# Four weight loads in place of nine, in a fused attention and feed-forward kernel

## The chip, the cores and the metric

The kernel runs on one core of a Trainium2 chip. The metric is the device time of one execution in microseconds (us), as the median of several runs. A core has TensorE (PE: matrix products), VectorE (DVE), ScalarE (ACT), GpSimd (POOL) and SyncE (SP), each with its own program in a fixed order, and 16 DMA engines that all of its queues share.

## The reference

All tensors are float32. There are 8 batches, 12 heads, 448 positions and 64 elements per head.

```python
def rmsnorm(x, g):
    return x / np.sqrt(np.mean(x * x, axis=-1, keepdims=True) + 1e-06) * g
q_n, k_n = rmsnorm(q, g_q), rmsnorm(k, g_k)
scores = np.matmul(q_n, k_n.transpose(0, 1, 3, 2)) / np.sqrt(64)
attn = exp(scores - max) / (sum of the row + 1e-9)
attn_out = np.matmul(attn, v)                                    # (8, 12, 448, 64)
x = attn_out.transpose(0, 2, 1, 3).reshape(3584, 768)
h = x @ w_in                                                     # w_in  (768, 2048)
g = h * np.clip(h + 3.0, 0.0, 6.0) / 6.0
out = g @ w_out                                                  # w_out (2048, 768)
```

## The kernel before

**Units of work.** Two heads make a pair; six pairs are a batch, 48 pairs in all, handled in order. Loads of q, k and v go by groups of two pairs (GP = 2): 384 KB for the first 384 positions of a tensor, in rows of 768 B, and smaller DMAs for the last 64 positions, in rows of 256 B. They land in rings of three groups (`kq_in`, `v_st`). After the first groups, SP issues all of them (L281 to L300), so that they share one hardware queue, which the profile calls q1.

**A pair's way through attention.** GpSimd squares q and k (L334; ScalarE does it for the first pairs), VectorE sums the squares (L337), ScalarE makes the reciprocal root for both pairs of a group (L345, L348), GpSimd normalizes into bf16 (`qk`, L353). The result is transposed: on TensorE for pairs 0 to 13 (L367, then copied by L385 and L303), by a DMA afterwards (L377). TensorE makes scores (L395, L402), ScalarE their exponentials (L408), TensorE the weighted sums of v (L429, L435), VectorE divides (L445, L446), and the result, transposed again, goes into `xT`.

**The feed-forward part.** For each batch, `h_item` makes 16 row blocks of h, transposed, with six products each (L479, 448 columns, over the six 128-row blocks of w_in). ScalarE (L485) and VectorE (L490) apply the gate and write `gT`. `y_item` makes output tiles: 16 products each over w_out's sixteen 128-row blocks (L498), 384 of the 768 columns at a time. One block of batch 0 (`h_early`) goes product by product as each pair's `xT` comes. The attention of the next batches and the feed-forward of the earlier ones are mixed on TensorE.

**What sets the order.** A planner (`Plan`) runs a small model of the engines while the kernel is built and puts every instruction into its engine's program. At run time each engine follows that order and waits where an operand is not there. The model books every DMA in one file, `pipe`: a DMA takes its size divided by RATE (270 bytes per ns) behind the one before it, and is taken to have landed LAND = 1700 ns later. `dma_transpose` books 1.4 times its size. An operation is placed when its operands are there by this model, by its key; feed-forward items fill TensorE by the shares in `share`.

**The weights.** They lie in HBM as float32 and are cast to bf16 by the DMA itself, issued by GpSimd (the software queue, q0). w_in comes by columns in five DMAs (256, 256, 512, 512 and 512 columns); w_out in four, each of eight 128-row blocks and one half of the columns. The lists say after which group's v load a DMA may be issued, and then columns or blocks:

```python
W_IN = ((2, 0, 256), (2, 256, 256), (2, 512, 512), (3, 1024, 512), (3, 1536, 512))
W_OUT = ((5, 0, 0, 8), (5, 0, 8, 8), (6, 1, 0, 8), (7, 1, 8, 8))
```

`h_item` waits for the w_in DMA that holds its 128 columns. `y_item` waits for the two DMAs of its half of w_out's columns, and for the first batch the output tiles stand in an order that uses the first half of the columns for two tiles before the second half.

Of the kernel before, what the change touches and what calls it, by code (L numbers as in the profile page):

```python
# [63 lines left out]
class Plan:  # L64
# [3 lines left out]

    HOP = 60
    PRICE, FAIR = {"POOL": 0.5, "ACT": 2.0, "DVE": 1.5}, 0  # L70
    ISSUE, LAND, RATE = {"SP": 600, "ACT": 600, "POOL": 900}, 1700, 270.0

    STEADY, SLACK, EARLY = 110e3, 500, 3000

# [6 lines left out]
    def add(self, key, ways, deps=(), lag=0, size=0, hold=False):  # L81
        op = Op(key, ways, deps, lag, size)
        op.left += hold
        self.todo += 1
        if op.left == 0:
            self.known.append(op)
        return op

    def dma(self, key, n, size, fn, deps=(), queue="SP", hold=False):

        op = self.add(key, [(queue, self.ISSUE[queue] * n, fn)], deps, self.LAND, size, hold)
        op.load = True
        return op

    def dma_transpose(self, key, size, fn, deps):
        return self.add(key, [("SP", 1270, fn)], deps, 2100, 1.4 * size)

    def item(self, lane, place, count, ns, fn, deps):

# [89 lines left out]
def kernel(  # L189
# [11 lines left out]
    nc = tc.nc  # L201

    B, H, S, D = q.shape
    DM, DFF = moe_w_in.shape
    P = 128
    NT = S // P
# [4 lines left out]
    NKT = DM // P  # L211
# [4 lines left out]
    GP = 2  # L216
    NV, NK, NX, NE, NQ = 4, 4, 3, 8, 3
    YC = 384
# [33 lines left out]
    w_out_sb = const.tile([P, NFT, DM], BF16, name="w_out_sb")  # L252
# [7 lines left out]
    plan = Plan(share=(2.0, 1.0, 0.65, 3.0, 0.45))  # L260
# [51 lines left out]
    def load_w_in(c, n):  # L312
        nc.gpsimd.dma_start(out=w_in_sb[:, :, c:c + n],
                            in_=moe_w_in[:, c:c + n].rearrange("(kt p) f -> p kt f", p=P))

    def load_w_out(half, f, n):
        cols = slice(half * YC, (half + 1) * YC)
        nc.gpsimd.dma_start(out=w_out_sb[:, f:f + n, cols],
                            in_=moe_w_out[f * P:(f + n) * P, cols].rearrange("(ft p) m -> p ft m", p=P))


    def which(part):
# [172 lines left out]
    def y_mm(b, t, c, n, f, m):  # L495

        c0 = (0 if b % 2 == 0 else S + REST) + t * P if t < NT else FULL
        nc.tensor.matmul(  # L498
            out=m[:, 0:n], lhsT=gT[:, f, c0:c0 + P], rhs=w_out_sb[:, f, c:c + n],
            start=(f == 0), stop=(f == NFT - 1),  # L500
        )

    def y_copy(eng, c, n, m, ys):
        copy(eng, out=y_r[ys][:, c:c + n], in_=m[:, 0:n])

    def y_store(b, t, ys, cols):
        y = y_r[ys][:, cols]
        if t < NT:
            rows = out[b * S:b * S + FULL, cols].rearrange("(p t) m -> p t m", t=NT)
            nc.sync.dma_start(out=rows[:, t, :], in_=y)  # L510
        else:
            nc.sync.dma_start(out=out[(b - 1) * S + FULL:b * S, cols], in_=y[0:REST])
            nc.sync.dma_start(out=out[b * S + FULL:(b + 1) * S, cols], in_=y[REST:P])
# [58 lines left out]
    h_ops, gates, y_ops, stores = {}, {}, {}, []  # L572

    def h_item(b, f):
        deps = [w_in_op(f)] + px[HP * b:HP * b + HP]

        deps += y_ops.get(b - 2, [])[-1:] + (y_rest.get(b - 1, []) if b % 2 == 0 else [])
        it = plan.item("h", b + f / NFT, NKT, 189, lambda kt, m: h_mm(b, f, kt, m), deps)
        h_ops.setdefault(b, []).append(it.ops[-1])
        n = len(gate_ops)  # L580
        t = t_r[n % len(t_r)]
        r = add((0, 0), [("ACT", 550, lambda: relu(it.bank[0], t))],
                [it.ops[-1]] + gate_ops[n - len(t_r):n - len(t_r) + 1] * (n >= len(t_r)))
        it.out = add((0, 0), [("DVE", 600, lambda: gate(b, f, it.bank[0], t))], [r])
        gates.setdefault(b, []).append(it.out)
        gate_ops.append(it.out)

    def h_early(f):

        m, t, mm = m_r[f], t_r[f], None  # L590
        for kt in range(NKT):
            mm = add((kt + 2, 2), [("PE", 189, lambda kt=kt: h_mm(0, f, kt, m))],
                     [px[kt], mm, w_in_op(f)], 165)
        h_ops.setdefault(0, []).append(mm)
        r = add((0, 0), [("ACT", 550, lambda: relu(m, t))], [mm])
        out = add((0, 0), [("DVE", 600, lambda: gate(0, f, m, t))], [r])
        gates.setdefault(0, []).append(out)
        gate_ops.append(out)
        plan.banks.append([m, out])

    def y_item(b, t, c, n, place, alone=False):

        part = c // YC
        deps = [*w_out_ops[part], *gates[b], *(gates[b - 1] if t == NT else [])]
        it = plan.item("y", place, NFT, 3 + n / 2.4, lambda f, m: y_mm(b, t, c, n, f, m), deps)
        y_ops.setdefault(b, []).append(it.ops[-1])
        if t == NT:
            y_rest.setdefault(b, []).append(it.ops[-1])
        if (b, t) not in y_rows:
            y_rows[b, t] = (len(y_rows), [])  # L610
        k, parts = y_rows[b, t]
        ys = k % len(y_r)
        it.out = add((0, 1), [("ACT", 160 + 0.83 * n, lambda: y_copy(A_, c, n, it.bank[0], ys)),
                              ("DVE", 160 + 1.04 * n, lambda: y_copy(V, c, n, it.bank[0], ys))],
                     [it.ops[-1]] + ([stores[k - len(y_r)]] if k >= len(y_r) else []))
        parts.append(it.out)
        if alone:
            plan.dma((-1, 0), 1, P * n * 4, lambda: y_store(b, t, ys, slice(c, c + n)), [it.out])
        elif len(parts) == DM // YC:
            stores.append(plan.dma((-1, 0), 1 if t < NT else 2, P * DM * 4,  # L620
                                   lambda: y_store(b, t, ys, slice(0, DM)), parts))

    def feed_forward(b):

        if b:
            ts = (NT, *range(NT)) if b % 2 == 0 else range(NT)
            ys = [(t, c) for t in ts for c in range(DM // YC)]
            if b == 1:
                ys = [(0, 0), (1, 0), (0, 1), (1, 1), (2, 0), (2, 1)]
            for i, (t, c) in enumerate(ys):  # L630
                last = b == B and t == NT - 1
                for j in range(2 if last and c else 1):
                    n = YC // 2 if last and c else YC
                    y_item(b - 1, t, c * YC + j * n, n, b + YLAG + (i + j / 2) / len(ys), last)
        if b < B:
            for f in range(NFT):
                h_early(f) if b == 0 and f < 1 else h_item(b, f)

    gate_ops, y_rows, y_rest = [], {}, {}
    QA, VL, WK = 1, 1.5, 0  # L640
    YLAG = 0.12


    W_IN = ((2, 0, 256), (2, 256, 256), (2, 512, 512), (3, 1024, 512), (3, 1536, 512))
    W_OUT = ((5, 0, 0, 8), (5, 0, 8, 8), (6, 1, 0, 8), (7, 1, 8, 8))
    w_loads, w_in_ops, w_out_ops = [], [], ([], [])
    for i, (after, *cols) in enumerate(W_IN):
        op = plan.dma((GP * after - WK, 3 + i), 1, NKT * P * cols[1] * 4, lambda cols=cols: load_w_in(*cols),
                      queue="POOL", hold=True)
        w_loads.append((after, op))  # L650
        w_in_ops.append((sum(cols), op))
    for i, (after, *rows) in enumerate(W_OUT):
        op = plan.dma((GP * after - WK, 8 + i), 1, rows[2] * P * YC * 4, lambda rows=rows: load_w_out(*rows),
                      queue="POOL", hold=True)
        w_loads.append((after, op))
        w_out_ops[rows[0]].append(op)

    def w_in_op(f):
        return next(op for end, op in w_in_ops if f * P < end)
# [16 lines left out]
    for p in range(NPAIR):  # L676
        g = p // GP
        if p % GP == 0:
# [6 lines left out]
            for p0, n in todo:  # L685
                lk.append(plan.dma((p0, 0), 3, n * kb, lambda p0=p0, n=n: load_k(nc.sync, p0, n), old))
                eng, queue = (nc.scalar, "ACT") if g < QA else (nc.sync, "SP")
                lq.append(plan.dma((p0, 1), 2, n * kb, lambda p0=p0, n=n, eng=eng: load_q(eng, p0, n), old,
                                   queue=queue))
# [10 lines left out]
            for i in range(GP):  # L700
                j, p0 = min(i, len(todo) - 1), p + i
                parts = []
                for part in ((0, 1) if p0 == 0 else (2,)):
                    m = len(squares)
                    n = 2 if part == 2 else 1
# [95 lines left out]
    x_stage(NPAIR - 1)  # L801
    plan.banks += [[x[:, 0], d_ops[i - 2]] for i, x in enumerate(sc_r)]
    feed_forward(B - 1)
    feed_forward(B)
    with tc.manual_schedule(engines=set(ENGINES.values())):
        plan.run()
# [31 lines left out]
```

## Time and profile before

| | |
|---|---|
| median of 3 runs | 439.57 us (438.73 to 439.68) |
| the profiled execution | 439.38 us, of which the span of the core 437.6 us |
| TensorE busy | 409.8 us (94% of the span) |
| ScalarE, VectorE, GpSimd busy | 254.3, 234.7, 195.2 us |
| DMA packets | 126506, 64.55 MB |
| software queue (q0, the weights) | 8144 packets, 6.29 MB, 9.2% of 16 engines' span |

The weight DMAs, as the trace has their issue (us from the span's start) and the time to landing:

| | issued at | us to landing |
|---|---|---|
| w_in columns 0 to 256, to 512, to 1024 | 28.7, 29.6, 30.4 | 8.3, 11.0, 15.8 |
| w_in columns to 1536, to 2048 | 35.5, 36.4 | 16.2, 21.6 |
| w_out, first half of the columns | 39.1, 40.0 | 25.0, 30.3 |
| w_out, second half of the columns | 63.6, 75.2 | 13.2, 10.7 |

In the slices of the page, 40 to the span, a digit is the busy share in tenths, 9 for 90% or more. A DMA's packets are told with the bytes that were written, so that a row of weights that is cast counts half of what is read. Times of packets of two queues on one engine can overlap: a share over 100% is possible. In a timeline row, "x2" means two instructions told together, with the time of both.

### The profile page before, as it was taken

How to read it: one execution, taken by the hardware profiler on the slowest of the kernel's cores; microseconds unless marked ns; L12 is line 12 of the kernel's file. 1: busy time of each engine (PE TensorE's matmuls, PEld its weight loads, DVE VectorE, ACT ScalarE, POOL GpSimd, SP SyncE). 2: the span in 40 equal slices, each digit the busy share in tenths (PEclk: the TensorE clock that was granted, in tenths of full speed). 3: DMA queues.
4: the chain of work that ended last, by engine and by line, in shares of the span. 5: the costliest groups of instructions: out<-in, count | busy, mean ns of one | idle time of the engine just before them, and what ended most of it. 6: DMA issues, size and time to landing. Idle time of an engine off the chain costs nothing.

```text
span 437.6 us, 8944 instructions
## 1 busy us (share of the span) xinstructions
PE 409.8 (94%) x3520; PEld 236.5 (54%) x3520; DVE 234.7 (54%) x492; ACT 254.3 (58%) x414; POOL 195.2 (45%) x146
## 2 busy tenths in 40 slices
PE   0677899999999998999999999999999999999997
PEld 0355565555566554555555555555565555555565
DVE  6486777766455557556466366344444253343322
ACT  3886887734877885968778587666643032132100
POOL 3697785596377776859676556311000000000000
PEclk9998999999999999999999999999999999999999
DMA  6999999995978898999999994333211201100022
GB/s 170 267 228 216 221 222 239 250 190 131 237 161 190 204 217 189 201 219 194 227 212 167 191 213 121 73 88 91 61 24 49 72 1 51 59 36 37 25 85 73
DMA packets 126506, 64.55 MB, mean 148 GB/s; under 512 B 77824, under 2 KB 123008, under 8 KB 126464
## 3 DMA queue, kind: packets, MB, share of 16 engines
q1 hardware_dynamic: 117488, 57.24, 57.5%
q0 software_dynamic: 8144, 6.29, 9.2%
q8 instruction: 27, 0.44, 0.4%
q10 hardware_dynamic: 832, 0.46, 0.4%
q14 instruction: 15, 0.12, 0.1%
HBM read 45.61 MB, written 11.01 MB: 129 GB/s over the span
## 4 chain that ended last, share of the span: by engine, by line
PE 82%; DMA 7%; ACT 3%; DVE 3%; SPq 2%; POOL 2%; issue 1%; ACTq 0%; POOLq 0%
PE m L479 18%; PE m L498 17%; PE t_ps L498 9%; PE t_ps L479 8%; PE av L435 7%; PE sc L395 6%; PE sc L498 6%; PE sc L479 4%; DMA kq_in<-in_k_dram 3%; DMA kq<-qk 3%; PE av L429 2%; DMA kq_in<-in_q_dram 2%; PE sc L402 2%; ACT eT L408 2%; DVE ssq L337 1%
## 5 line engine op out<-in xcount | busy, mean ns | idle before, releaser
L408 ACT ACTIVATE eT<-sc 128x896 bf16<-128x896 f32 x168 | 147.2, 915 | 42.2 <-PE sc L395 38.5
L498 PEld LDWEIGHTS <-gT 128*128 128x128 bf16 x912 | 85.5, 98 | 61.7 <-issue 8.9
L479 PE MATMUL m<-xT,w_in_sb 128*128 128x448 bf16 x486 | 109.9, 353 | 1.7 <-DVE xT L475 0.6
L479 PEld LDWEIGHTS <-w_in_sb 128*128 128x128 bf16 x768 | 70.7, 98 | 68.8 <-issue 12.0
L353 POOL TENSOR_TENSOR qk<-kq_in,rstd 128x1024 bf16<-128x1024 f32 x47 | 89.0, 1903 | 41.6 <-DMA kq<-qk 20.8
L498 PE MATMUL m<-w_out_sb,gT 128*128 128x384 bf16 (+1 forms) x480 | 87.3, 324 | 0.0
L334 POOL TENSOR_TENSOR sq<-kq_in 128x1024 f32<-128x1024 f32 x41 | 77.2, 1894 | 13.0 <-DMA kq_in<-in_q_dram 3.6
L490 DVE SCALAR_TENSOR_TENSOR gT<-t_sb,m 128x448 bf16<-128x448 f32 x81 | 49.9, 618 | 41.8 <-ACT t_sb L485 41.4
L485 ACT ACTIVATE t_sb<-m 128x448 f32<-128x448 f32 x81 | 44.1, 546 | 47.9 <-PE m L479 47.2
L337 DVE TENSOR_REDUCE ssq<-sq 128x16 f32<-128x1024 f32 (+1 forms) x49 | 58.1, 1190 | 9.5 <-POOL sq L334 7.5
L435 PE MATMUL av<-vaug,eT 128*128 128x65 bf16 x1152 | 59.6, 196 | 0.0
L435 PEld LDWEIGHTS <-eT 128*128 128x128 bf16 x1152 | 52.8, 100 | 7.2 <-issue 1.6
L498 PE MATMUL t_ps<-w_out_sb,gT 128*128 128x384 bf16 x256 | 46.9, 326 | 0.0
L395 PE MATMUL sc<-kq 64*128 64x448 bf16 x288 | 41.6, 363 | 4.0 <-ACT eT L408 2.5
L429 PE MATMUL av<-vaug,eT 128*128 128x130 bf16 x192 | 43.0, 224 | 2.4 <-ACT eT L408 1.2
L479 PE MATMUL t_ps<-xT,w_in_sb 128*128 128x448 bf16 x192 | 44.5, 352 | 0.7 <-DVE gT L490 0.7
L303 POOL CAST vaug<-v_st 128x512 bf16<-128x512 f32 x33 | 20.3, 620 | 55.0 <-PE av L435 46.6
L445 DVE RECIPROCAL rden<-av 128x4 f32<-128x4 f32 x96 | 17.3, 180 | 48.8 <-PE av L435 47.1
L446 DVE TENSOR_TENSOR xn<-av,rden 128x256 bf16<-128x256 f32 x96 | 40.7, 424 | 3.3
L374 ACT ACTIVATE kq<-kq,gprime 128x448 bf16<-128x448 bf16 x34 | 22.8, 670 | 14.2 <-DMA kq<-qk 14.2
L498 PE MATMUL sc<-w_out_sb,gT 128*128 128x384 bf16 (+1 forms) x176 | 29.1, 319 | 0.0
L485 ACT ACTIVATE t_sb<-t_ps 128x448 f32<-128x448 f32 x32 | 17.5, 547 | 19.7 <-PE t_ps L479 18.5
(50 smaller groups left out, 225.0 us busy)
## 6 DMA issues: line engine op xcount, KB each, us to landing
v_st<-in_v_dram SPq DMA_DIRECT2D x24, 384.0 KB, 4.7
kq_in<-in_k_dram SPq DMA_DIRECT2D x23, 384.0 KB, 4.5
kq_in<-in_q_dram SPq DMA_DIRECT2D x23, 384.0 KB, 4.8
out_dram<-y_sb SPq DMA_DIRECT2D x23, 384.0 KB, 2.6
w_out_sb<-in_moe_w_out_dram POOLq DMA_DIRECT2D x4, 768.0 KB, 19.1
w_in_sb<-in_moe_w_in_dram POOLq DMA_DIRECT2D x3, 768.0 KB, 16.2
out_dram<-y_sb SPq DMA_DIRECT2D x9, 192.0 KB, 2.7
v_st<-in_v_dram SPq DMA_DIRECT2D x48, 32.0 KB, 4.3
```

The source lines that it names most:

```text
L334: eng.tensor_tensor(out=sq, in0=x, in1=x, op=A_MULT)
L337: nc.vector.tensor_reduce(out=ssq_r[(p // GP) % 2][:, p % GP, :, which(part)].rearrange("p h a t -> p h (a t)"), in_=sq_r[m][:, :, which(p ...
L353: eng.tensor_tensor(out=qk_r[p % NQ][:].rearrange("p a t h d -> p h (a t) d"), in0=raw(p, 2), in1=rstd_r[(p // GP) % 2][:, p % GP].rearran ...
L395: nc.tensor.matmul(out=sc[:, h, 0:S], lhsT=kT_r[p % NK][rows, t * P:(t + 1) * P], rhs=qT_r[p % NK][rows], start=True, stop=True,)
L408: nc.scalar.activation(out=e2_r[d % NE][:, :, 0:S], in_=sc_r[i][:, :, 0:S], func=EXP, bias=0.0, scale=1.0,)
L429: nc.tensor.matmul(out=av, lhsT=rest[:, cols], rhs=va[:, 3].rearrange("p h d -> p (h d)"), start=True, stop=False, skip_group_check=True,)
L435: nc.tensor.matmul(out=av[:, h * W:(h + 1) * W], lhsT=e[t][h][:, cols], rhs=va[:, t, h], start=False, stop=(t == NT - 1 and h == 1), skip_ ...
L446: nc.vector.tensor_tensor(out=xn_r[p % NQ][:, t].rearrange("p n (h d) -> p n h d", h=2), in0=av4[:, :, :, 0:D], in1=rden.unsqueeze(3).to_b ...
L479: nc.tensor.matmul(out=m[:, 0:S], lhsT=w_in_sb[:, kt, f * P:(f + 1) * P], rhs=xT[:, kt, b % NX, x_slot(b)], start=(kt == 0), stop=(kt == N ...
L485: nc.scalar.activation(out=t[:], in_=m[:, 0:S], func=RELU, bias=0.5, scale=1.0 / 6.0,)
L490: nc.vector.scalar_tensor_tensor(out=gT[:, f, (b % 2) * S:(b % 2 + 1) * S], in0=t[:], scalar=1.0, in1=m[:, 0:S], op0=A_MIN, op1=A_MULT,)
L498: nc.tensor.matmul(out=m[:, 0:n], lhsT=gT[:, f, c0:c0 + P], rhs=w_out_sb[:, f, c:c + n], start=(f == 0), stop=(f == NFT - 1),)
```

## The change

Weights come in four DMAs: w_in in two halves of its columns (rows of 4096 B read, 2048 written), w_out in two halves of its row blocks with all columns (3072 B read, 1536 written). All of w_out may be issued after group 5. An output tile waits for both w_out DMAs, and the first batch's output tiles stand in the common order. The planner books 310 bytes per ns, 3000 ns more until a GpSimd DMA has landed, four fifths of the weights' size and 1.25 times that of a transpose.

```diff
-    ISSUE, LAND, RATE = {"SP": 600, "ACT": 600, "POOL": 900}, 1700, 270.0
+    ISSUE, LAND, RATE = {"SP": 600, "ACT": 600, "POOL": 900}, 1700, 310.0
+    SHARED = 3000
...
-        op = self.add(key, [(queue, self.ISSUE[queue] * n, fn)], deps, self.LAND, size, hold)
+        op = self.add(key, [(queue, self.ISSUE[queue] * n, fn)], deps, self.LAND + self.SHARED * (queue == "POOL"), size, hold)
...
-        return self.add(key, [("SP", 1270, fn)], deps, 2100, 1.4 * size)
+        return self.add(key, [("SP", 1270, fn)], deps, 2100, 1.25 * size)
...
-    def load_w_out(half, f, n):
-        cols = slice(half * YC, (half + 1) * YC)
-        nc.gpsimd.dma_start(out=w_out_sb[:, f:f + n, cols],
-                            in_=moe_w_out[f * P:(f + n) * P, cols].rearrange("(ft p) m -> p ft m", p=P))
+    def load_w_out(f, n):
+        nc.gpsimd.dma_start(out=w_out_sb[:, f:f + n, :],
+                            in_=moe_w_out[f * P:(f + n) * P, :].rearrange("(ft p) m -> p ft m", p=P))
...
-        part = c // YC
-        deps = [*w_out_ops[part], *gates[b], *(gates[b - 1] if t == NT else [])]
+        deps = [*w_out_ops, *gates[b], *(gates[b - 1] if t == NT else [])]
...
-            if b == 1:
-                ys = [(0, 0), (1, 0), (0, 1), (1, 1), (2, 0), (2, 1)]
...
-    W_IN = ((2, 0, 256), (2, 256, 256), (2, 512, 512), (3, 1024, 512), (3, 1536, 512))
-    W_OUT = ((5, 0, 0, 8), (5, 0, 8, 8), (6, 1, 0, 8), (7, 1, 8, 8))
-    w_loads, w_in_ops, w_out_ops = [], [], ([], [])
+    W_IN = ((2, 0, 1024), (3, 1024, 1024))
+    W_OUT = ((5, 0, 8), (5, 8, 8))
+    w_loads, w_in_ops, w_out_ops = [], [], []
...
-        op = plan.dma((GP * after - WK, 3 + i), 1, NKT * P * cols[1] * 4, lambda cols=cols: load_w_in(*cols),
+        op = plan.dma((GP * after - WK, 3 + i), 1, NKT * P * cols[1] * 4 * 4 // 5, lambda cols=cols: load_w_in(*cols),
...
-        op = plan.dma((GP * after - WK, 8 + i), 1, rows[2] * P * YC * 4, lambda rows=rows: load_w_out(*rows),
+        op = plan.dma((GP * after - WK, 8 + i), 1, rows[1] * P * DM * 4 * 4 // 5, lambda rows=rows: load_w_out(*rows),
...
-        w_out_ops[rows[0]].append(op)
+        w_out_ops.append(op)
```

## The prediction

> **What bounds the kernel now.** I read the page's engine totals first, then its slices, then the windows around the weight loads.
>
> ```profile
> PE 409.8 (94%) x3520; PEld 236.5 (54%) x3520; DVE 234.7 (54%) x492; ACT 254.3 (58%) x414; POOL 195.2 (45%) x146
> ```
>
> ```profile
> PE   0677899999999998999999999999999999999997
> ...
> DMA  6999999995978898999999994333211201100022
> ```
>
> TensorE is the bound: 409.8 of 437.6 us busy, 27.8 idle. The change leaves its work alone, so it can move the time only through that idle time. The DMA engines are full in the first 24 slices (to some 260 us). The weights travel between about 31 and 86 us, so I looked there, in windows of 10 us:
>
> ```profile
> core 0: us, PE busy (x) PEld busy (x) DVE busy (x) ACT busy (x) POOL busy (x), PEclk, DMA share, GB/s
> 30.00:40.00 10.00, 7.83 (x98) 5.27 (x96) 6.30 (x16) 6.35 (x12) 9.98 (x9) 0.83 1.17 203
> 40.00:50.00 10.00, 8.03 (x106) 5.16 (x105) 6.70 (x18) 8.22 (x13) 6.54 (x6) 1.00 1.19 224
> 50.00:60.00 10.00, 9.50 (x108) 5.67 (x107) 8.21 (x19) 8.18 (x14) 7.44 (x7) 1.00 1.21 221
> ```
>
> TensorE idles 2.17 + 1.97 + 0.50 = 4.6 us here, and is full afterwards, but for 2.9 us between 160 and 180 and 1.2 between 210 and 230. What the change can win is therefore some 4 us here, and up to 4.1 later if the order happens to fall better.
>
> The next view decides the case: packets, MB and share of 16 engines of the software queue (q0, the weights) and the hardware queue (q1, all of SP's loads), in windows with one size of weight row each: 32 to 35 us (512 B written), 40 to 50 (1024 B), 62 to 68 (768 B).
>
> ```profile
> q0 software_dynamic: 626, 0.32, 80.1%
> q1 hardware_dynamic: 425, 0.24, 36.7%
> ```
> ```profile
> q0 software_dynamic: 1369, 1.38, 81.1%
> q1 hardware_dynamic: 1367, 0.84, 37.3%
> ```
> ```profile
> q0 software_dynamic: 969, 0.74, 78.2%
> q1 hardware_dynamic: 1043, 0.59, 44.9%
> ```
>
> And 86 to 89 us, with no weights under way:
>
> ```profile
> q1 hardware_dynamic: 1374, 0.74, 101.9%
> ```
>
> One packet of q0 goes for one of q1: 1369 against 1367, whatever their sizes. q1 moves 458 packets per us alone and 137 beside 1024-B weight rows. A packet of the trace is one row: 0.32 MB/626 = 511 B. So q, k and v are held to the weights' row rate, and a longer weight row makes that rate lower.
>
> **Where the loads stand.** The last q load of pairs 10 and 11 is issued at 33.6 and 34.3 us (KB, us to landing):
>
> ```profile
> kq_in<-in_q_dram SPq DMA_DIRECT2D x1, 384.0 KB, 12.5
> kq_in<-in_q_dram SPq DMA_DIRECT2D x1, 64.0 KB, 13.5
> ```
>
> It lands at 34.3 + 13.5 = 47.8. GpSimd squares these pairs next, normalizes them, and TensorE transposes pair 10 at 58.35:
>
> ```profile
> 48.70 3.74 POOL L334 TENSOR_TENSOR sq<-kq_in 128x1024 f32<-128x1024 f32 x2
> ...
> 55.62 3.76 POOL L353 TENSOR_TENSOR qk<-kq_in,rstd 128x1024 bf16<-128x1024 f32 x2
> ```
> ```profile
> 58.35 0.61 PE L367 MATMUL t_ps<-identity,qk 128*128 128x128 bf16 x8
> ```
>
> The slack along this is 0.9 us (47.8 to 48.70) and, on TensorE, 58.35 − 57.5 (end of pair 10's normalize, half of 3.76 after 55.62) = 0.85.
>
> **The change, part by part.**
>
> *Fewer packets.* Weight rows number 6×128×5 + 4×8×128 = 7936 before; after, 2×768 + 2×1024 = 3584. Time per packet, from the shares: 0.801×3×16 us/626 = 61 ns (512 B), 0.782×6×16/969 = 77 (768 B), 0.811×10×16/1369 = 95 (1024 B), so 0.067 ns per byte. The sizes 2048 and 1536 B do not occur; on the line they take 165 and 130 ns. From below they are bounded by being cut into rows of 1024 and 768 B (second rival); from above by two of the smaller ones, 190 and 154. I take the line, since three sizes lie on it. Engine time falls from 0.092×437.6 = 40 us (the page's q0 share) to (1536×165 + 2048×130)/16/1000 = 32.5. This is the gain, and it is 7.5 us of queue, not of TensorE.
>
> *The price on q, k and v.* A pair of packets, one of each queue, takes 160 us/1369 = 117 ns per engine with 95 ns of weight, and 96/969 = 99 with 77: the weight packet plus 22. After: 187 ns for w_in, 152 for w_out. Each w_in half then flows 768×187/16 = 9.0 us, each w_out block 1024×152/16 = 9.7. From the first weight packet at 31.1, with all four issued back to back, they land at 40.1, 49.1, 58.8 and 68.5. Before, w_out's third and fourth piece went out at 63.6 and 75.2 and left room. Meanwhile q1 gets 16/0.187 = 86 packets per us until 49.1, then 105.
>
> From 31.1 to 47.8 before, q1 moved 2609 packets to land pair 10's q. After: 1536 by 49.1, the other 1073 at 105 per us: 59.3, which is 11.5 us later. For pairs 12 and 13 (landed 59.1, 4272 packets): 3579 by 68.5 and 693 at 458 per us: 70.0, 10.9 later. So one delay serves both.
>
> Squaring starts at 59.4 instead of 48.70: +10.7. Less the 0.85 of slack, TensorE's transposes of pair 10 come 9.8 us late. TensorE runs in program order; behind those transposes stand pair 10's scores, w_in's remaining products, and all else. At that point 29 of w_in's first 96 products have run. The planner cannot hold pair 10 back, as it does not know the delay: its pipe is one file, and it books pair 10's loads just behind the first half (2.52 MB/310 = 8.1 us; the three pieces before were 11.7), not between the packets of the next three DMAs. I take +9.8. If the order puts ahead the 19 further products that the first half allows, 19×0.189 = 3.6 us are filled: 6.2; if the 21 that ran from 50 to 58.3 (189 ns apart in a row) come behind instead, 4.0 more: 13.8.
>
> *Waiting for whole halves.* The first product of w_in ran at 37.11, as the 256-column piece landed (28.7 + 8.3). With the half at 40.1, the three products run by then move: 3×0.189 = +0.6. The main run, from 49.44, has its half, and the second half at 49.1 comes before its first use. w_out's last row at 68.5 is ahead of the first product at 86.97, so its merged dependence and the changed order of the first output tiles cost nothing. If the weights came 18 us later, that cover would be gone and every further us would count.
>
> *Issues on GpSimd.* Nine of about 0.87 us become four: 4.3 us less, 1.7 of it at 28.7, ahead of normalizing pairs 6 and 7. GpSimd is full there (9.98 of 10). Between 0 and −1.7; most of that idles again waiting for the sums, so −0.5.
>
> *The clock.* At 30 to 40 us it reads 0.83: (1 − 0.83)×10/0.5 = 3.4 us at half speed, after stretches of waiting. A wait of 10 us may bring one more: between 0 and 1.7 us; I take +1.0, for part of that stretch may fall on further waiting. The Trainium skill, "TensorE: Matmul & The Clock Gate", Part 1, has the array at half rate until some 3.4 us of sustained work; by that, an estimate, the whole 1.7 is paid and the sum below would be 0.7 higher. The 0.83 agrees with its length, and no row here shows a wait of 10 us.
>
> *The planner's rates* (310 for 270, transposes 1.25) reorder everything behind. The idle 4.1 us of 160 to 230 may vanish or double: ±4, taken as 0.
>
> Sum, against the profiled execution's 439.38: + 9.8 + 0.6 − 0.5 + 1.0 = 450.3. The median of the runs is 0.2 above that execution: **450.5**.
>
> **Rivals.**
>
> 1. *Faster: the engines don't share row by row.* If several rows of q1 answer one of 2048 B, q, k and v keep their pace and the 7.5 us of saved queue time comes to them. Then the idle time at 30 to 50 us (4.1) goes: 439.6 − 4.1 = 435.5. It decides where q1 holds some 137 rows per us beside the long rows. The near equal counts at two sizes, and q1's lag at the third, speak against it; that no row is as long as 2048 B leaves it open. A better order could give the same. The Trainium skill, "DMA: Bandwidth & Descriptors", section Queues, rings and completion order, says that an engine drains a whole packet of typically 9 to 17 descriptors before it turns to the next queue row. By that rule a longer row need not change the turns, which is this rival; the trace differs, with one row for one.
> 2. *The packets stay small.* Cut to 1024 and 768 B, they leave q1 at 137 per us: 2609/137 = 19.0, landing at 50.1, 2.3 late and 1.4 past the squaring's start; 0.85 of that is slack, and the first half lands at 42.3, so 4×0.189 = 0.8: 441.
> 3. *Slower by less: the order covers it.* If it puts the 19 further products that the first half allows ahead of pair 10, 19×0.189 = 3.6 us of the wait is filled; all 67 left would fill it. 440 to 447.
>
> **How the numbers follow.** The forecast gets 0.60 (its own range 443 to 456: 6.2 without the clock and with 1.7 for GpSimd, less a little for the order, to 13.8 with the whole 1.7), rival 1 0.20, rivals 2 and 3 0.10 each. 437 to 457 leaves out most of rival 1 and little else. Within 0.2% (about 0.9 us, what a measurement of this kernel can tell from no change) lie edges of rivals 1 to 3: 0.04. Faster: 0.19; slower: 0.77.
>
> **What would show it.** Software packets of 2048 and 1536 B near 165 and 130 ns; q1 near 86 and 105 per us beside them; pair 10's q landing near 59; TensorE idle some 10 us more between 50 and 75; all weights in by 70. Wrong if q1 keeps 130 per us or more, or if TensorE is busy through 75 us.

## The result and the profile after

The median is 456.26 us (4 runs, 453.17 to 465.66), against 439.16 us for the kernel before. The ratio is 1.036, with a 95% interval of 1.031 to 1.040; it leaves out the run of 465.66, whose granted clock was lower than that of the others (0.974 against 0.984 and 0.985). The profiled execution took 457.8 us, its span 456.0. The change makes the kernel slower, by more than the forecast of 450.5.

The engine totals of after, in the page:

```profile
PE 412.5 (90%) x3520; PEld 237.2 (52%) x3520; DVE 238.7 (52%) x498; ACT 249.7 (55%) x406; POOL 195.2 (43%) x143
```

TensorE is busy 2.7 us more, and idle 43.5 us in place of 27.8. To see where, both kernels in the same stretches, first before, then after (busy us of each engine, then the granted clock of TensorE, DMA share and GB/s; from 75 to 110 us TensorE is full in both):

```profile
30.00:75.00 45.00, 40.30 (x490) 25.35 (x488) 33.18 (x80) 34.76 (x55) 33.14 (x26) 0.96 1.21 219
...
110.00:300.00 190.00, 185.91 (x1732) 105.34 (x1731) 107.61 (x218) 141.51 (x228) 115.85 (x77) 1.00 0.87 182
```
```profile
30.00:75.00 45.00, 33.16 (x372) 20.41 (x373) 29.50 (x67) 27.13 (x47) 29.70 (x20) 0.85 1.10 218
...
110.00:300.00 190.00, 178.19 (x1673) 99.63 (x1671) 108.37 (x218) 136.01 (x220) 121.89 (x81) 1.00 0.85 180
```

The 18.4 us of added span are 7.1 us of idle time between 30 and 75 us (45 − 33.16 against 45 − 40.30), 7.7 between 110 and 300 (11.8 against 4.1), 0.9 before 30, and the 2.7 of longer busy time, which goes with the clock of 0.85. So there are two losses, one where the weights travel and one long after they are in.

The first loss. Packets, MB and share of the two queues in after, at 32 to 38 us (rows of 2048 B) and 56 to 72 us (1536 B):

```profile
q0 software_dynamic: 483, 0.99, 91.5%
q1 hardware_dynamic: 402, 0.16, 15.1%
```
```profile
q0 software_dynamic: 1675, 2.54, 86.8%
q1 hardware_dynamic: 1676, 0.96, 27.6%
```

One for one still holds: 1676 against 1675. Equal totals alone would also fit turns of several rows each; but the counts stay close even in 0.3 us, in which one engine moves only some 1.5 rows of each queue (24 and 28 from 46.7 us in after). q1 has 1676/16 = 105 packets per us beside rows of 1536 B and 402/6 = 67 beside 2048 B, where 458 per us went alone. (At 32 to 38 us it does not use all its turns; what keeps it from that was not tried.) What that does to GpSimd, whose program runs in order (start, us, what, idle time before and what ended it):

```profile
37.69 1.89 POOL L334 TENSOR_TENSOR sq<-kq_in 128x1024 f32<-128x1024 f32 x1 [4.82 <-DMA kq_in<-in_q_dram]
39.54 3.76 POOL L353 TENSOR_TENSOR qk<-kq_in,rstd 128x1024 bf16<-128x1024 f32 x2
43.24 0.89 POOL L314 DMA_DIRECT2D w_in_sb<-in_moe_w_in_dram  x1
...
62.25 1.89 POOL L334 TENSOR_TENSOR sq<-kq_in 128x1024 f32<-128x1024 f32 x1 [4.33 <-DMA kq_in<-in_q_dram]
64.10 3.76 POOL L353 TENSOR_TENSOR qk<-kq_in,rstd 128x1024 bf16<-128x1024 f32 x2
```

And TensorE in the same time:

```profile
41.50 1.03 PE L367 MATMUL t_ps<-identity,qk 128*128 128x128 bf16 x8 [4.76 <-POOL qk L353]
...
66.06 1.03 PE L367 MATMUL t_ps<-identity,qk 128*128 128x128 bf16 x8 [3.39 <-POOL qk L353]
```

GpSimd stands 4.8 us on the squares of pair 8. The last q load of that pair, issued at 28.0 us, takes 9.5 us and lands at 37.5; before, it was issued at 27.9 and took 3.8. Queued behind the squares are the normalizing of pairs 6 and 7, which TensorE wants to transpose, and the second w_in DMA. At 62 us the same happens again: the squares of pair 12, whose q load lands at 62.0 in place of 59.1, hold back the normalizing of pair 10. TensorE waits 4.76 and 3.39 us. Within each wait the clock drops, and it stays at half for 6.8 us:

```profile
37.80:44.60 6.80, 3.06 (x22) 2.31 (x22) 2.81 (x7) 1.37 (x2) 6.78 (x5) 0.50 1.06 250
65.10:71.90 6.80, 5.84 (x38) 3.37 (x39) 5.12 (x13) 0.90 (x2) 4.61 (x3) 0.50 1.15 219
```

The second loss. Who waited longest on ScalarE between 75 and 300 us, before and then after (us in total, times, longest):

```profile
ACT kq L374 <- DMA kq<-qk: 14.2, 11, 2.8
```
```profile
ACT kq L374 <- DMA kq<-qk: 23.3, 17, 2.7
```

ScalarE scales a pair's transposed q, and stands there for the transposing DMA. Exponentials queue behind it, and TensorE waits for those. One such place in after, first ScalarE, then TensorE:

```profile
181.49 0.67 ACT L374 ACTIVATE kq<-kq,gprime 128x448 bf16<-128x448 bf16 x1 [2.16 <-DMA kq<-qk]
```
```profile
183.02 0.54 PE L402 MATMUL sc<-kq 128*128 128x448 bf16 x2 [2.12 <-ACT eT L408]
```

In between, from 182.07, ScalarE makes the exponentials. The same happens at 208.35 and 209.87 us (1.98 and 1.75 us of waiting). Of TensorE's late idle time in after, 9.4 us are waits for exponentials, against 3.5 before.

### The profile page after: what moved, and what is told of

It reads as the page before. It is cut to its first block, busy times and chain, and to the rows that moved or that the text cites. A ratio compares the mean times of both kernels' runs of the same rounds, so it can differ in the third digit from the quotient of the medians.

```text
span 456.0 us, 8932 instructions
## 1 busy us (share of the span) xinstructions
PE 412.5 (90%) x3520; PEld 237.2 (52%) x3520; DVE 238.7 (52%) x498; ACT 249.7 (55%) x406; POOL 195.2 (43%) x143
## 4 chain that ended last, share of the span: by engine, by line
PE 55%; DMA 23%; POOL 8%; SPq 6%; issue 4%; ACT 2%; DVE 2%; ACTq 0%; POOLq 0%
PE m L498 13%; PE m L479 12%; DMA kq_in<-in_q_dram 9%; DMA kq<-qk 9%; PE sc L498 6%; PE t_ps L479 5%; PE t_ps L498 5%; POOL sq L334 5%; PE sc L479 5%; DMA v_st<-in_v_dram 4%; PE av L435 4%; PE sc L395 3%; POOL qk L353 2%; SPq L293 2%; ACT eT L408 1%
## 5 line engine op out<-in xcount | busy, mean ns | idle before, releaser
L479 PE MATMUL m<-xT,w_in_sb 128*128 128x448 bf16 x468 | 106.2, 356 | 0.5 <-DVE gT L490 0.5
L334 POOL TENSOR_TENSOR sq<-kq_in 128x1024 f32<-128x1024 f32 x43 | 81.0, 1893 | 28.0 <-DMA kq_in<-in_q_dram 24.4
L498 PE MATMUL m<-w_out_sb,gT 128*128 128x384 bf16 x480 | 87.7, 326 | 0.0
L490 DVE SCALAR_TENSOR_TENSOR gT<-t_sb,m 128x448 bf16<-128x448 f32 x78 | 47.9, 618 | 47.8 <-ACT t_sb L485 47.5
L485 ACT ACTIVATE t_sb<-m 128x448 f32<-128x448 f32 x78 | 42.1, 544 | 43.7 <-PE m L479 42.6
L435 PE MATMUL av<-vaug,eT 128*128 128x65 bf16 x1152 | 59.1, 195 | 0.0
L429 PE MATMUL av<-vaug,eT 128*128 128x130 bf16 x192 | 42.8, 223 | 7.3 <-DVE xn L446 4.2
L498 PE MATMUL t_ps<-w_out_sb,gT 128*128 128x384 bf16 x256 | 47.9, 326 | 0.0
L479 PE MATMUL t_ps<-xT,w_in_sb 128*128 128x448 bf16 x186 | 42.9, 353 | 0.0
L304 POOL CAST vaug<-v_st 128x512 bf16<-128x512 f32 x33 | 21.3, 649 | 48.7 <-PE av L435 39.1
L304 DVE COPY y_sb<-m 128x384 f32<-128x384 f32 x26 | 14.5, 556 | 32.5 <-PE m L498 32.4
L367 PE MATMUL t_ps<-identity,qk 128*128 128x128 bf16 x112 | 11.1, 259 | 20.9 <-DVE qk L353 11.8
## 6 DMA issues: line engine op xcount, KB each, us to landing
w_in_sb<-in_moe_w_in_dram POOLq DMA_DIRECT2D x2, 1536.0 KB, 14.2
```

The source lines that it names most:

```text
L334: eng.tensor_tensor(out=sq, in0=x, in1=x, op=A_MULT)
L429: nc.tensor.matmul(out=av, lhsT=rest[:, cols], rhs=va[:, 3].rearrange("p h d -> p (h d)"), start=True, stop=False, skip_group_check=True,)
L435: nc.tensor.matmul(out=av[:, h * W:(h + 1) * W], lhsT=e[t][h][:, cols], rhs=va[:, t, h], start=False, stop=(t == NT - 1 and h == 1), skip_ ...
L479: nc.tensor.matmul(out=m[:, 0:S], lhsT=w_in_sb[:, kt, f * P:(f + 1) * P], rhs=xT[:, kt, b % NX, x_slot(b)], start=(kt == 0), stop=(kt == N ...
L485: nc.scalar.activation(out=t[:], in_=m[:, 0:S], func=RELU, bias=0.5, scale=1.0 / 6.0,)
L490: nc.vector.scalar_tensor_tensor(out=gT[:, f, (b % 2) * S:(b % 2 + 1) * S], in0=t[:], scalar=1.0, in1=m[:, 0:S], op0=A_MIN, op1=A_MULT,)
```

## The experiments

Two theories of the two losses had to be told apart. The first: the long rows slow q, k and v and cost the early loss, while the planner's new order has a cost of its own. The second: the rows alone do it all, the late idle time being the early delay carried on. Times are medians, ratios are to the kernel before on the same chip.

**Rows and order, separately.** The first two kernels cross them. Old order, long rows:

```diff
     def load_w_in(c, n):
+        if c not in (0, 1024):
+            return
+        n = 1024
...
     def load_w_out(half, f, n):
-        cols = slice(half * YC, (half + 1) * YC)
+        if half:
+            return
+        cols = slice(0, DM)
```

> The planner of before, unchanged, so that every engine keeps its order of before; but the first w_in slot moves columns 0 to 1024, the fourth the other 1024, and the two first w_out slots move eight row blocks with all columns each; the other five slots issue nothing. Theory (long rows hold q, k and v to about 80 packets per us, and the new order has a cost of its own): pair 10's q lands near 59 us, idle TensorE time and half clock between 30 and 75 us grow by 8 to 11 us, nothing is added behind 110 us: 447 to 450 us. Rival A (rows alone do all of it, the late idle time too): 454 to 458. Rival B (the order alone does it): 437 to 441.

New order, short rows (the DMA calls inside the loops, with the loops' columns, are left out here):

```diff
     def load_w_in(c, n):
+        for c, n in ((0, 256), (256, 256), (512, 512)) if c == 0 else ((1024, 512), (1536, 512)):
...
     def load_w_out(f, n):
+        for c in (0, YC):
```

> The planner and the slots of after, but each slot issues its columns or blocks as before did: w_in in 256, 256, 512, 512 and 512 columns, w_out in halves of the columns (rows of 512, 1024 and 768 B written), so 9 DMAs of 0.87 us on GpSimd in 4 slots. Theory: q1 keeps 130 to 190 packets per us beside the weights, the idle time at 30 to 75 us is near that of before (5 to 8 us), the 7.7 us more behind 110 us stay: 445 to 449 us. Rival A (rows alone): 438 to 441. Rival B (order alone): 454 to 458.

Measured: 451.07 us (ratio 1.030, 1.024 to 1.035) and 450.29 us (1.029, 1.022 to 1.036). Either part alone costs some 12 us (before took 438.27 there), 1 us more than the upper end of what was expected; together they cost 16 to 17, so they overlap. The stretches of the old order with long rows:

```profile
30.00:75.00 45.00, 31.03 (x341) 18.64 (x339) 22.71 (x55) 24.39 (x38) 23.67 (x17) 0.81 1.11 222
...
110.00:300.00 190.00, 186.75 (x1701) 105.44 (x1700) 110.38 (x217) 140.43 (x229) 123.53 (x79) 1.00 0.88 186
```

and of the new order with short rows:

```profile
30.00:75.00 45.00, 35.42 (x415) 21.72 (x413) 31.03 (x70) 28.75 (x48) 36.21 (x26) 0.92 1.21 219
...
110.00:300.00 190.00, 178.69 (x1670) 100.15 (x1669) 108.89 (x220) 135.92 (x217) 119.88 (x80) 1.00 0.83 176
```

In the old order the long rows add 9.3 us of idle time before 75 us and none behind 110 (3.2 against 4.1). In the new order, short rows keep nearly all of the late loss (11.3 of 11.8). So the late idle time is no early delay carried on; the second theory is out. The early loss is of both: 4.9 us of idle time from the new order with short rows, 7.1 with long ones. That is more than the first theory allowed: with short rows the early idle time was expected at 5 to 8 us, and is 9.6. GpSimd stands 3.6 us on pair 12's squares there too, and TensorE's longest wait is

```profile
64.12 0.98 PE L369 MATMUL t_ps<-identity,qk 128*128 128x128 bf16 x8 [2.67 <-POOL qk L355]
```

against 3.39 us with long rows. The wait of 4.76 us is gone: pair 8's squares run at 33.92 us without one, and TensorE has smaller waits of 1.79 and 1.56 elsewhere (34.00 and 49.13). So in the new order the long rows make the first wait, and most of the second is there without them.

The old order with long rows also shows how the early loss comes about there (TensorE):

```profile
42.55 0.56 PE L484 MATMUL m<-xT,w_in_sb 128*128 128x448 bf16 x1 [6.38 <-DMA w_in_sb<-in_moe_w_in_dram]
62.53 2.40 PE L484 MATMUL m<-xT,w_in_sb 128*128 128x448 bf16 x6 [3.95 <-DVE gT L495]
```

The first product of w_in waits 6.38 us for the whole half, and everything behind it on TensorE with it. Then 3.95 us go at the time at which pair 10's q, here landed at 58.6 us, is squared (from 58.81) and summed (from 60.74); the gate on VectorE, which TensorE waits for, stands behind that sum (61.87). Together the two waits are 10.3 us, near the lateness of that load (58.6 − 47.8 = 10.8), which fits that a wait already paid is not paid twice. So "long rows" in this kernel stands for two things, slower q loads and the wait for a whole half of w_in; for w_in, no run has the one without the other.

**The planner's rates.** Four kernels change only the two numbers, or one of them, in after or in before:

```diff
 # after with the old rates: RATE 310.0 -> 270.0, transposes 1.25 -> 1.4
 # before with the new rates: RATE 270.0 -> 310.0, transposes 1.4 -> 1.25
 # before, RATE alone: 270.0 -> 310.0
 # before, transposes alone: 1.4 -> 1.25
```

> After, but RATE back at 270 and transposes at 1.4 times their size in the planner; the four loads, SHARED and the four fifths stay. Theory (the late idle time comes from the planner's faster pipe): the early loss stays, the late 7.7 us mostly go: 446 to 451 us. Rival (the late idle time is the early delay, carried on): 454 to 458.

> Before, but with RATE 310 and transposes at 1.25 times their size in the planner; the nine loads stay as they were. Theory: no more wait at 30 to 75 us than 2 us over before, but 4 to 8 us more idle TensorE time behind 110 us: 443 to 448 us. Rival (the late idle time is the early delay, carried on): 438 to 441.

> Before, with RATE 310 and transposes at 1.4 times their size. Both rates together cost 12.7 us, the transposes' booking alone 3.9. Theory (the loads' rate is the larger part, since pairs are put at the times at which their loads are booked to land): 446 to 450 us, TensorE waiting 3 to 9 us more behind 75 us. Rival (the two act only together): 438 to 441.

> Before, with transposes booked at 1.25 times their size in place of 1.4, RATE at 270. If the transposes' booking (11% less) is the part of the rates that costs, 446 to 451 us, with the added waits behind 75 us, where transposes begin; if the loads' rate is, or both together, 438 to 442.

| | us | ratio (95%) | idle 30 to 75, 75 to 110, 110 to 300 us |
|---|---|---|---|
| before | 439.16 | | 4.7, 0.0, 4.1 |
| before, new rates | 450.93 | 1.031 (1.024 to 1.039) | 5.0, 4.0, 8.5 |
| before, RATE 310 | 448.87 | 1.023 (1.019 to 1.027) | 4.6, 3.9, 8.6 |
| before, transposes 1.25 | 442.92 | 1.008 (1.005 to 1.011) | 5.4, 0.0, 6.4 |
| after | 456.26 | 1.036 (1.031 to 1.040) | 11.8, 0.0, 11.8 |
| after, old rates | 456.79 | 1.042 (1.036 to 1.048) | 15.5, 3.0, 5.1 |

On the loads of before, both new rates together end 3 us above the upper end expected, with 4.4 us more idle time behind 110, as expected, and 4.0 between 75 and 110, which was not; and this with no early loss (5.0 against 4.7). RATE alone costs what was expected, and the transposes' booking alone some 4 us, in neither of the ranges that were set for it but nearer the lower. RATE is the larger part. On after's loads the expectation missed on the time, which lies in the rival's range: with the old rates the late idle time falls from 11.8 to 5.1 us, as expected (and against the rival's reason), but 6.7 us come back before 110. There two waits stand out on TensorE (30 to 110 us):

```profile
PE m L479 <- DVE gT L490: 7.7, 1, 7.7
PE sc L402 <- ACT eT L408: 5.1, 1, 5.1
```

while GpSimd's squares wait 18.5 us for q loads. So going back to the old rates wins nothing in after. As these waits read, the long rows' early loss depends on what happens to be queued behind the waiting pair, and the old rates place it worse. The planner's other changes (SHARED, the four fifths and the slots) were not tried by themselves.

**Is the old order just lucky?** A kernel with a hardly changed rate, and one with a rate too slow:

```diff
-    ISSUE, LAND, RATE = {"SP": 600, "ACT": 600, "POOL": 900}, 1700, 270.0
+    ISSUE, LAND, RATE = {"SP": 600, "ACT": 600, "POOL": 900}, 1700, 272.0    # the other: 250.0
```

> Before, with RATE 272 in place of 270 in the planner and nothing else: some part of the order falls otherwise, for no reason of the hardware. Theory (the cost of the new order is that of a pipe booked too fast): 437 to 441 us, idle TensorE time behind 110 us within 2 us of before's 4.1. Rival (the order of before is a lucky one, and any other order costs about as much as the rates did): 446 to 452 us.

> Before, with RATE 250: the planner books a slower pipe than before, by 8%. Theory (a pipe booked too fast makes engines wait at run time, one booked too slow only moves work back in the order): 434 to 441 us, idle TensorE time behind 110 us 1 to 4 us. Rival (270 is a sharp optimum, found by trying, and any move off it costs): 443 to 448.

Measured: 437.59 us (ratio 0.997, 0.994 to 1.000) and 438.21 us (0.999, 0.996 to 1.001). Both times are as expected: two other orders cost nothing, and the three in which the planner books a faster pipe or faster transposes (310, 1.25, both) do. How the cost grows between 272 and 310 was not tried. ScalarE's wait for transposed pairs between 75 and 300 us mostly goes with RATE: at 250, then at 310 (it was 14.2 us at 270 and 10.3 at 272):

```profile
ACT kq L374 <- DMA kq<-qk: 4.1, 5, 1.5
```
```profile
ACT kq L374 <- DMA kq<-qk: 21.5, 12, 4.3
```

TensorE's idle time behind 110 us goes along: 0.25 at 250, which is less than the 1 to 4 us expected, then 4.1 at 270, 2.1 at 272 and 8.6 at 310. At 250 the time is no better, as TensorE idles 6.2 us between 30 and 75 and 3.2 between 75 and 110.

**One weight at a time, in the old order.** Only `load_w_in`, or only `load_w_out`, gets the edit shown above.

> Before's order; w_in in two halves with rows of 2048 B in the first and fourth slot, w_out as before with 768 B. Theory: q1 at 84 per us until w_in is in (about 50 us), then 165: pair 10's q lands at 54 to 56 us in place of 47.8 (58.6 with all rows long), w_out comes sooner: 443 to 448 us. Rival (w_out's early long rows do the harm): 438 to 441.

> Before's order; w_in as before, w_out in two DMAs of eight blocks with all columns (1536 B) in the first two slots. Theory: until 57 us as before, then q1 at 105 per us in place of 160 until w_out is in, some 77 us; the loads of pairs 12 to 15 land 3 to 6 us later, where the order has slack: 439 to 444 us. Rival: 448 to 452, if w_out's rows are the part that costs.

Measured: 446.82 us (1.019, 1.015 to 1.024) and 440.08 us (1.005, 1.001 to 1.009), both times as expected. Pair 10's q lands at 54.4 and 47.9 us. With w_in long, TensorE's longest wait is 7.5 us for the half of w_in. With w_out long, q of pairs 12 and 13 lands at 59.8 in place of 59.1, q of pairs 14 and 15 at 80.9 in place of 77.4, and the kernel pays 2 us: these loads have more slack.

**Turns, by row and by queue.** Shorter rows of w_in, in the old order:

```diff
     def load_w_in(c, n):
+        for c in range(c, c + n, 256):    # each 256 columns a DMA
```

> Before's planner and order; all of w_in in DMAs of 256 columns (rows of 512 B written), two in each of the slots that moved 512 columns; w_out as before. Theory (q, k and v go at the weights' row rate): q1 at 190 to 210 packets per us until w_in is in, some 63 us; pair 10's q lands near 45 us in place of 47.8; w_in's last columns 5 us later: 436 to 440 us, the early idle time 2 to 5 us. Rival (the weights' bytes are what matters): as before, 438 to 440, q1 at 135 per us beside them.

And the old order with long rows, q loads of groups 4 to 8 on ScalarE's queue:

```diff
     def load_q(eng, p, n):
+        eng = nc.scalar if 4 <= p // GP <= 8 else eng
```

> The kernel with before's order and long rows, but the q loads of groups 4 to 8 are issued by ScalarE, so that they have a hardware queue of their own (q10). Theory (an engine turns from queue to queue, one packet each): beside rows of 2048 B q1 and q10 together move 130 to 160 packets per us in place of 80, q of pairs 10 and 11 land before 54 us, and more than half of the 12 us comes back: 440 to 446 us, unless ScalarE is held up by its issues. Rival (the long rows take the engines' bandwidth as such): 449 to 453.

Packets of the queues at 38 to 46 us, with rows of 512 B and then with the second hardware queue:

```profile
q0 software_dynamic: 1626, 0.81, 74.1%
q1 hardware_dynamic: 1611, 0.93, 53.4%
```
```profile
q0 software_dynamic: 592, 1.18, 77.6%
q1 hardware_dynamic: 589, 0.39, 20.7%
q10 hardware_dynamic: 589, 0.33, 13.4%
```

Both are what turns of one packet per queue give: 1611 packets in 8 us are 201 per us beside rows of 512 B, and with three queues each has the same 589 to 592, so that q, k and v have 147 per us beside rows of 2048 B in place of 84. The gains went otherwise. With rows of 512 B the kernel takes 439.36 us (1.001, 0.999 to 1.004), as both the theory and its rival had it: pair 10's q lands at 47.1 and not near 45, as it is issued 1 us later; q of pairs 12 and 13 lands at 54.9 in place of 59.1, and nothing is won, since GpSimd squares these pairs only at 60.6. With the second queue it takes 458.59 us (1.045, 1.039 to 1.050) in place of less than 446. Pair 10's q lands at 49.2, as expected, but TensorE still waits 5.6 us for the half of w_in, and ScalarE, which now issues loads in its program's order, stands still ahead of one. It issues loads at 66.31 and 67.54 us, and then (start, us, idle before; the profile names a v load, which this operation does not read, so what held the issue at 66.31 stays open):

```profile
68.19 0.54 ACT L491 ACTIVATE t_sb<-m 128x448 f32<-128x448 f32 x1 [7.82 <-DMA v_st<-in_v_dram]
```

No version here beats before by more than the 0.3% of RATE 272, whose interval ends at 1.000.

## Why the prediction was right or wrong

*Direction and sharing: right.* The time rose, and the engines share row by row as forecast. Software packets have 2048 and 1536 B, with 67 and 105 packets per us left to q1 (86 and 105 were forecast); where q1 used all its turns beside 2048 B, in the old order with long rows at 36 to 47 us, it had 922/11 = 84:

```profile
q0 software_dynamic: 922, 1.86, 89.1%
q1 hardware_dynamic: 922, 0.51, 21.7%
```

The long rows alone move the time from 438 to 451 in the old order, the one that the prediction worked with. Rivals 1 and 2, other turns and small packets, fall by the packet counts and sizes, and rival 3 by the time, with two long waits that nothing filled.

*Packet times: small misses.* From the shares, 0.868×16×16/1675 = 133 ns for 1536 B (130 forecast), and for 2048 B 0.915×6×16/483 = 182 in after and 0.891×11×16/922 = 170 in the old order (165 forecast); the line was a little short at its far end.

*"With all four issued back to back" failed.* The second w_in DMA stood behind pair 8's squares on GpSimd, until 43.2 us. That left q1 alone from 42.8 to 46 us, when it moved 1207 packets. So pair 10's q did not land at 59.3 but at 46.8, a little sooner than before (47.8), all weights were in at 77.7 and not at 68.5, and the q loads that were waited for were those of pairs 8 and 12, not 10. The path on which the +9.8 rests is not the one that after took. In the old order, where GpSimd issues without that wait, pair 10's q landed at 58.6: there the forecast path is what ran.

*The early sum: close, by luck.* Measured: +7.1 idle between 30 and 75 and +2.7 busy, 9.8 against the 10.9 of the sum. But the waits are others, and 4.9 of the 7.1 us come with the new order and short rows too, which the sum does not hold. The clock was under-sized (1.0, bounds 0 to 1.7): two waits gave two half-speed stretches of 6.8 us, where before had one of 3.4. No run shows the −0.5 for GpSimd's issues by itself. That w_out's merged dependence costs nothing came true: w_out was in at 77.7, and its first product ran at 96.4.

*"The three products run by then move" was wrong reasoning.* In a program in order, the first product does not move, it holds all behind it. It showed as 6.38 us in the old order. In after it did not, since its first product ran at 47.07, past the landing at 42.7.

*The planner's rates, "±4, taken as 0": the term that failed.* Behind 110 us, where the forecast had nothing, after idles 7.7 us more, which is above the term's bounds and more than the 5.8 us between forecast and result. That it has a sign could have been argued from the profile before: ScalarE already waited 14.2 us for transposes there, and a faster booking would be expected to lengthen such waits. On the loads of before the two rates cost some 13 us by themselves. It is no price to be added, though: in after, the old rates take the late idle time away and the time stays at 457. So 456 inside 437 to 457, at its upper end and just above the 443 to 456 of the forecast itself, is a right direction with a sum whose terms came out otherwise.

## What to carry to other kernels

Where two queues share the DMA engines packet by packet, a longer row in the one slows the other, even as the total gets cheaper: here rows of 512 to 2048 B left 201 to 84 packets per us. Look at whose packets are waited for before lengthening those beside them; that long rows for the awaited traffic would pay was not tried, and shorter rows of weights won nothing here. In an order fixed ahead of time, a transfer booked too fast costs real waits, because the engine that stands there holds back work that is ready. A merged load must be priced from the landing of its last byte, with all that is queued behind its first reader. And a change of the planner's numbers is a change of its own: try it on the old loads before it is taken as 0.

## What the runs showed of the hardware

An engine gives one packet to each queue with work, by turns, whatever their sizes: two queues at 512, 768, 1024, 1536 and 2048 B, three queues at 2048 B. q1's rate beside those rows was 201, 164 (655 packets from 56 to 60 us of before), 137, 105 and 84 packets per us.

TensorE's clock fell to half 1.1 and 2.4 us into the two long waits of after, and came back 3.1 us after the first had ended (41.50 to 44.6) and 5.8 us after the second (66.06 to 71.9). The Trainium skill, "TensorE: Matmul & The Clock Gate", Part 1, puts the return at some 3.4 us of sustained work; the first is near that, the second took longer, though TensorE was busy for all of the 5.84 us. The traces show more: all half-speed stretches that ended before 400 us, in all kernels here, last 3.4, 6.8 or 10.2 us, whole steps of 3.4. In the steps of after around the second wait, TensorE was busy 0.98 of 3.41 us ahead of the drop (61.69 to 65.10), 2.44 of 3.40 in the first half-speed step (65.10 to 68.50), and all of 3.41 in the second (68.52 to 71.93), behind which the clock came back. After the first wait a step with 3.06 of 3.41 busy was enough (41.21 to 44.62). By these rows the second took longer because the work began 1 us into a step; where between 2.44 and 3.06 the bound lies was not looked for.
